# Two separate tiles for the odd pairs' arrays, second products in another order, and weight units in 11 stages: one change to a performer-and-two-MoE kernel on Trainium2

## The chip, the cores and the metric

The kernel runs on one core of one Trainium2 chip. The metric is the device time of one execution in microseconds (us). The core's engines run their own instruction streams and meet through semaphores: PE (TensorE, matrix products; PEld is its weight load), DVE (VectorE), ACT (ScalarE), POOL (GpSimd) and SP (SyncE, which here issues the transfers).

## The reference

What is computed, cut to what matters:

```python
attn = performer_attention(q, k, v, omega)            # 4 x 8 heads x 576 tokens x 64
x = attn.transpose(0, 2, 1, 3).reshape(2304, 512)
h = x @ w_in                                          # 512 -> 2048
x = (max(h, 0) + alpha * min(h, 0)) @ w_out           # first layer, 2048 -> 512
h = x @ w2_in
out = max(h, 0) ** 2 @ w2_out                         # second layer, same sizes
```

All is fp32. The matrix unit is used with operands rounded to a shorter format (`fp32r`), so each fp32 operand is kept as a rounded part (names with `h`) and a remainder (names with `l`), and a product is made of three matmuls: h x h, h x l and l x h.

## The kernel before

**Tiling.** The attention comes first and leaves `x` (512 x 2304) in memory. Then 2304 tokens are taken as three blocks of 768, each block as two halves of 384 (`HB`). The 2048 features are eight pairs of 128-row tiles. A *turn* is one pair of one block of the first layer.

**First products.** In block 0 of the first layer, `plain(p)` makes the four (feature half i, token half l) results of a pair in eight steps, one `multiply` (6 matmuls of 384 columns) each. From block 1 on, `pair(layer, p)` makes them in seven steps, with a scheme of seven products on sums of the quarters (`PRODUCTS`). It adds the seven products up in two PSUM arrays, `a` and `b`: products 1, 6, 7, 4 go to `a`, products 2, 5, 3 to `b`. Between them ACT copies `a` out (`copied`), and DVE adds such a copy to `b` (`plus`, tile `c`).

**Features.** The results pass through `activate` (first layer; ACT makes `n` and `r`, DVE puts them together with the slope `alpha`) or `square` (second layer). What follows is deferred: each step calls `catch_up()` once, which works off a list `behind` in stages. First comes "high": DVE computes the value and ACT rounds it into `gh`, at the next `catch_up`. Then comes "low": DVE makes the remainder `gl`, one `catch_up` later. All engines take their instructions in the order in which the code issues them.

**Second products of the first layer.** `mm2` multiplies the features of a turn with `w_out` during the next turn, in eight parts (half i = 1 first, four column groups c each); each part is 6 matmuls, of 512 and 256 columns. `FILL` says how many parts go behind each step m. The results add up over the eight turns of a block in six PSUM banks `y`, which `evacuate` empties when a block has ended (`COMPLETE` says which banks a part completes).

**Weights.** They arrive as 64-bit words and must be scaled, shifted, merged (ACT, DVE, POOL), summed for the seven-product scheme (`sums`), rounded (`cast1`, `cast2`, `cast3`) and given remainders (`rest1` to `rest3`), and are then written to HBM (`keep`) for the later blocks. The generator `made` does this in *units*: nine of the first layer, during the attention and block 0, and 16 of the second layer, eight each during blocks 1 and 2. Each unit is 18 stages (`STAGES`), and `upto` advances through them at a steady rate, behind each step of a turn: for the second layer's units 8 x 18 = 144 stages over the 49 steps of seven turns.

**The second layer.** `pair1` runs the seven products in an order in which product 1 of the next pair stands between 7 and 4. Even pairs take two tiles `h` for `a` and `b`; odd pairs take two banks of the tile `sumb`. The later `outer_products` (the second products of this layer, also with seven products) use `suma`, `sumb` and `sumc` as their sums; `combine` adds such a sum to `x` on DVE.

```python
a, b = (mp["ph"].tile([P, 512], F32, name="h")[:, :HB] for _ in range(2)) if p % 2 == 0 else (
    sums_of["b"][:, j, :HB] for j in range(2))
```

PSUM tiles and others are opened from pools with `reuse_waits="tile"`; the order of issue is written by hand, the waits are put in by the framework from the tiles that instructions read and write.

Of the kernel before, what the change touches and what calls it, by code (L numbers as in the profile page):

```python
# [9 lines left out]
F32 = mybir.dt.float32  # L10
# [8 lines left out]
P = 128  # L19
# [25 lines left out]
CAST = 11  # L45
STAGES = 18
DRAIN, DRAINED = 18, 6
# [5 lines left out]
def tile_performer_moe(ctx, tc, qt, kt, qn, kn, vn, omt, w1i, w1o, al, w2i, w2o, out):  # L53
# [100 lines left out]
    def made():  # L154
# [83 lines left out]
        for n, (n1, n2) in enumerate(UNITS):  # L238
            while n >= limit[0]:
                trail()  # L240
                yield
            todo = [[] for _ in range(STAGES)]
            if n1:

                plain = n1[0] == 0
                b0 = A21 if plain else A22
                a, b = used[n, 0, 0], used[n, 0, 1]
                todo[0] += [a.scale_high]
                todo[1] += [a.scale_low]
                todo[2] += [a.shift, b.scale_high]  # L250
                todo[3] += [lambda: merge(a), b.scale_low]
                todo[4] += [b.shift]
                todo[5] += [lambda: merge(b), lambda: cast1(n1, A11, S1)]
                todo[6] += [lambda: rest1(n1, A11, S1)]
                todo[7] += [lambda: cast1(n1, b0, A11)]
                todo[8] += [lambda: rest1(n1, b0, A11)]
                if not plain:
                    todo[8] += [lambda: keep(n1, 0, slice(0, 3), tiles["ma"])]
                todo[9] += [lambda: sums((1, 3))]
                todo[10] += [lambda: sums((2, 4))]  # L260
                todo[12] += [lambda: cast1(n1, S1, S3)]
                todo[13] += [lambda: rest1(n1, S1, S3), lambda: cast1(n1, S3, 8)]
                todo[14] += [lambda: rest1(n1, S3, 8)]
                if n == 0:
                    held.append(lambda n1=n1: keep(n1, 0, slice(0, 7), ring[0][0][:, :, A22:], nc.scalar))
                elif plain:
                    todo[14] += [lambda: keep(n1, 0, slice(0, 7), ring[n1[1] % 2][0][:, :, A22:])]
                else:
                    todo[14] += [lambda: keep(n1, 0, slice(3, 7), tiles["ms"])]
            todo[4] += [trail]  # L270
            todo[7] += [trail]
            if n2 and n2[0] == 1:
                a, b = used[n, 1, 1], used[n, 1, 0]
                todo[0] += [a.scale_high]
                todo[1] += [a.scale_low]
                todo[2] += [a.shift, b.scale_high]
                todo[3] += [lambda: merge(a), b.scale_low]
                todo[4] += [b.shift]
                todo[5] += [lambda: merge(b)]
                todo[7] += [lambda: sums((1, 3), True)]  # L280
                todo[8] += [lambda: sums((2, 4), True), lambda: cast3(0, 2)]
                todo[9] += [lambda: rest3(0, 2), lambda: cast3(2, 3)]
                todo[10] += [lambda: rest3(2, 3), lambda: keep3(n2[1], 0, 3)]
                todo[12] += [lambda: cast3(4, 6)]
                todo[13] += [lambda: rest3(4, 6), lambda: cast3(6, 8)]
                todo[14] += [lambda: rest3(6, 8), lambda: keep3(n2[1], 4, 8)]
            elif n2:
                raw = lambda i: used[n, 1, i]
                todo[8] += [lambda: raw(1).scale_high()]
                todo[9] += [lambda: raw(1).scale_low()]  # L290
                todo[10] += [lambda: raw(0).scale_high()]
                todo[11] += [lambda: raw(1).shift(), lambda: raw(0).scale_low()]
                todo[12] += [lambda: merge(raw(1))]
                todo[14] += [lambda: cast2(n2, 1)]
                todo[15] += [lambda: rest2(n2, 1)]
                todo[16] += [lambda: raw(0).shift()]
                todo[17] += [lambda: merge(raw(0)),
                             lambda: tail.extend([lambda n2=n2: cast2(n2, 0), lambda n2=n2: rest2(n2, 0)])]
            for stage in todo:
                for what in stage:  # L300
                    what()
                position[0] += 1
                yield
# [11 lines left out]
    making, fetches, stepping, held = [], [], [], []  # L315

    def onward(most, blk):

        ask(most, blk)
        next(making[0])  # L320

    def upto(where, most, blk):

        while position[0] < min(where, most * STAGES):
            onward(most, blk)
# [383 lines left out]
    def features(layer, p):  # L709
# [9 lines left out]
        def activate(i, l, c, psum=False):  # L719
# [9 lines left out]
            if halves[i][2] < 2:  # L729
                return  # L730

            def high():
                nc.vector.scalar_tensor_tensor(out=r, in0=n, scalar=al_sb[:, f:f + 1], in1=r, op0=ALU.mult, op1=ALU.add)  # L733
                nc.scalar.copy(out=gh[:, i], in_=r)  # L734
# [3 lines left out]

            behind[0].append((high, low))

        def square(i, l, c, psum=False):
# [5 lines left out]

            def high():
                if psum:
                    nc.vector.tensor_tensor(out=to, in0=r, in1=r, op=ALU.mult)  # L750
                else:
                    nc.vector.scalar_tensor_tensor(out=to, in0=c, scalar=0.0, in1=c, op0=ALU.max, op1=ALU.mult)
                if i and l:
                    nc.scalar.copy(out=g["h", p // 4][:, p % 4], in_=to)
# [5 lines left out]

            behind[0].append((high, low))

# [66 lines left out]

    behind = [[], []]  # L830

    def catch_up():

        high, low = behind
        for _, f in low:
            f()
        for f, _ in high:
            f()
        behind[:] = [], high

    def mm2(turn, p, gh, gl, y):

        w = ring[p % 2][1]
        for n, i in enumerate((1, 0)):
            first, last = turn == 0 and n == 0, turn == NPAIR - 1 and n == 1
            wh, wl = w[:, 0, i], w[:, 1, i]
            for c in range(KC):
                cs = slice(c * P, (c + 1) * P)
                for a0, a1 in cuts(c):
                    ts = slice(a0 - c * NB, a1 - c * NB)  # L850
                    for j, (u, v) in enumerate(((wh, gh), (wh, gl), (wl, gh))):
                        nc.tensor.matmul(  # L852
                            y[a0 // 512][:, a0 % 512:a0 % 512 + a1 - a0], u[:, cs], v[:, i, ts],
                            start=first and j == 0 and a0 % 512 == 0, stop=last and j == 2,
                            skip_group_check=True)
                yield

# [18 lines left out]

    FILL = {0: (0, 1, 1, 0, 3, 1, 2), 1: (0, 2, 2, 0, 3, 2, 3)}

    COMPLETE = {4: (0,), 5: (1, 2), 6: (3,), 7: (4, 5)}

# [25 lines left out]
    for n, (layer, k, turn, p) in enumerate(plan):  # L906
# [10 lines left out]
        for m, got in enumerate(steps, DRAINED if n == 0 else 0):  # L917
# [5 lines left out]
            if first and turn:  # L923

                upto((p + 1) * STAGES + STAGES * (m + 1) // 8 + 1, ENDS[0], 0)
            elif layer == 0 and k and turn:
                upto(ENDS[k - 1] * STAGES + 8 * STAGES * ((turn - 1) * 7 + m + 1) // 49, ENDS[k], k)
            elif layer == 0 and k and m == 6:
                ask(ENDS[k], k)
            elif (layer, k, turn) == (0, 1, 0) and m < 2:  # L930

                onward(ENDS[0], 0)
# [11 lines left out]
            full = []  # L944
            for _ in range(1 if first else FILL[layer][m]):
                part, _ = next(fill, (None, None))
# [18 lines left out]
    pz = ctx.enter_context(tc.tile_pool(name="pz", bufs=1, space=PSUM, reuse_waits="tile"))  # L965
    sums_of = {n: pz.tile([P, 2, 512], F32, name=f"sum{n}") for n in "bac"}
    ORDER = ((4, "c"), (1, "a"), (5, "b"), (6, "a"), (2, "c"), (7, "a"), (3, "c"))

    STATES = {4: (1, 1), 1: (0, 0), 5: (1, 1), 6: (1, 1), 2: (1, 0), 7: (0, 1), 3: (1, 0)}
    spread = {name: t.rearrange("p b n -> p (b n)")[:, :NB] for name, t in sums_of.items()}  # L970

    def slot_of(k, use):
        return (15 * k + use) % 2

    def pair1(k, p):

        a, b = (mp["ph"].tile([P, 512], F32, name="h")[:, :HB] for _ in range(2)) if p % 2 == 0 else (
            sums_of["b"][:, j, :HB] for j in range(2))
        w = ring[slot_of(k, p)][0]
# [35 lines left out]
    def outer_products(k, q, part, c_major=False, banks=None):  # L1015
# [3 lines left out]
        fresh = n not in (6, 7)  # L1019
        to = banks or [spread[name][:, c * QW:(c + 1) * QW] for c in range(3)]  # L1020
        h, l = g["h", part], g["l", part]
# [43 lines left out]
    def combine(k, n, name):  # L1065
        nc.vector.tensor_tensor(out=room_of(k, n), in0=spread[name], in1=room_of(k, n), op=ALU.add)  # L1066

# [63 lines left out]
    for k in range(BLOCKS):  # L1131
# [22 lines left out]
        for q in range(7):  # L1154
            for part in range(2):
# [10 lines left out]
                if (q, part) == (0, 0):  # L1166
                    for _ in range(2):
                        catch_up()
# [56 lines left out]
```

## Time and profile before

| | |
|---|---|
| time, median of 3 runs | 976.93 us (974.57 to 978.13) |
| the profiled execution | 975.11 us, span of its instructions 973.3 us |
| PE busy | 910.4 us, 94% of the span |
| DVE / ACT / POOL busy | 677.9 / 521.6 / 128.7 us |
| mean granted clock of TensorE | 0.993 |

Busy times of PE overlap, since matmuls are pipelined and their ends modelled: a matmul of 384 columns has a row of 0.34 us, while the next one can start after about half of that. A row of the profile gives the start in us from the span's start, the duration, the engine, the line of the kernel, the operation, what it writes and reads, and in brackets the idle time of the engine before it with the instruction that ended it. A row of a window gives its bounds and length, the busy us of PE, PEld, DVE, ACT and POOL with the number of their instructions, the granted clock, the busy share of the DMA engines and their GB/s.

The attention takes about the first 130 us; block 0 of the first layer lasts until about 270, blocks 1 and 2 until about 555, and the second layer takes the rest.

### The profile page before, as it was taken

The numbers are of one execution on the slowest core, as the hardware profiler recorded it, in microseconds if no ns is written. First come the engines' busy times: TensorE is split into PE (matmuls) and PEld (weight loads), VectorE is DVE, ScalarE is ACT, GpSimd is POOL, SyncE is SP. The second block draws the span as 40 slices with busy tenths as digits, with TensorE's granted clock in tenths as the row PEclk, the third lists the DMA queues.
The fourth block names the chain that finished last, engine by engine and source line by source line (L and its number), as shares of the span: only waits on it lengthen the run. The fifth ranks groups of instructions, "written<-read, shape, count | busy, mean of one in ns | idle before, by whom it ended". The sixth has DMA issues, their size and how long they took to land.

```text
span 973.3 us, 18463 instructions
## 1 busy us (share of the span) xinstructions
PE 910.4 (94%) x7328; PEld 834.2 (86%) x7328; DVE 677.9 (70%) x1071; ACT 521.6 (54%) x1109; POOL 128.7 (13%) x128
## 2 busy tenths in 40 slices
PE   9999999999999989899989888999988899988997
PEld 7998889888888878778878778889987899887997
DVE  5768878989877676776777754668745588446573
ACT  6888867767766665566665632235322245222341
POOL 6632203223101102101111100000000000000000
PEclk9999999999999999999999989999999999999999
DMA  8633336787558999548899655576776486865663
GB/s 296 198 106 114 111 141 214 262 290 280 187 184 290 325 344 351 182 172 322 302 360 351 252 184 176 181 270 250 252 246 211 156 310 220 298 202 179 271 250 108
DMA packets 81861, 228.81 MB, mean 235 GB/s; under 512 B 6128, under 2 KB 16752, under 8 KB 76400
## 3 DMA queue, kind: packets, MB, share of 16 engines
q1 hardware_dynamic: 81424, 225.77, 65.6%
q10 hardware_dynamic: 352, 1.87, 0.5%
q8 instruction: 58, 0.95, 0.4%
q14 instruction: 27, 0.22, 0.1%
HBM read 170.47 MB, written 57.15 MB: 234 GB/s over the span
## 4 chain that ended last, share of the span: by engine, by line
PE 45%; DVE 18%; ACT 15%; issue 4%; POOL 2%; DMA 2%; POOLq 0%; ACTq 0%; DVEq 0%
PE h L696 12%; PE sumb L696 9%; PE suma L1031 8%; PE sumc L1031 8%; PE y L852 5%; DVE r L733 4%; ACT gh L734 3%; PE sumb L1031 3%; ACT x L121 2%; DVE gl L737 2%; POOL wf L133 2%; DVE c L989 2%; ACT n L727 2%; ACT r L728 2%; DMA k<-ma 2%
## 5 line engine op out<-in xcount | busy, mean ns | idle before, releaser
L696 PE MATMUL h<-xh,w 128*128 128x384 f32 x1040 | 301.9, 341 | 12.6 <-DVE c L794 6.1
L696 PEld LDWEIGHTS h<-xh,w 128*128 128x128 f32 x1040 | 191.6, 189 | 26.2 <-DVE c L794 10.2
L852 PE MATMUL y<-gh,w 128*128 128x512 f32 (+1 forms) x768 | 212.5, 339 | 1.1 <-ACT gh L734 1.1
L696 PE MATMUL h<-xl,w 128*128 128x384 f32 x520 | 175.7, 338 | 0.9 <-DVE xl L374 0.9
L852 PEld LDWEIGHTS y<-gh,w 128*128 128x128 f32 x768 | 135.5, 189 | 15.9 <-DVE w L197 2.0
L852 PE MATMUL y<-gl,w 128*128 128x512 f32 (+1 forms) x384 | 132.2, 344 | 16.3 <-DVE gl L737 16.2
L133 POOL TENSOR_TENSOR wf<-x 128x512 int32<-128x512 int32 x64 | 79.3, 1240 | 367.1 <-DVE x L131 265.6
L696 PE MATMUL sumb<-xh,w 128*128 128x384 f32 x336 | 104.5, 358 | 24.9 <-DVE c L989 7.9
L1045 ACT CAST gh<-g 128x768 fp32r<-128x768 f32 x72 | 56.6, 833 | 84.9 <-PE suma L1031 38.7
L696 PEld LDWEIGHTS h<-xl,w 128*128 128x128 f32 x520 | 98.1, 189 | 4.5 <-DVE xl L374 1.4
L696 PEld LDWEIGHTS sumb<-xh,w 128*128 128x128 f32 x336 | 63.4, 193 | 39.8 <-DVE c L989 15.6
L852 PEld LDWEIGHTS y<-gl,w 128*128 128x128 f32 x384 | 72.5, 189 | 28.1 <-DVE gl L737 23.1
L1047 DVE TENSOR_TENSOR gl<-g,gh 128x768 fp32r<-128x768 f32 x72 | 65.8, 955 | 32.2 <-PE suma L1031 17.2
L734 ACT CAST gh<-r 128x768 fp32r<-128x768 f32 x48 | 40.1, 836 | 87.4 <-DVE r L733 87.4
L989 DVE TENSOR_TENSOR c<-sumb,s 128x384 f32<-128x384 f32 x24 | 13.4, 558 | 71.2 <-ACT s L985 45.4
L1031 PE MATMUL sumc<-w,gh 128*128 128x256 f32 x416 | 62.1, 286 | 0.0
L1031 PE MATMUL suma<-w,gh 128*128 128x256 f32 x448 | 58.1, 285 | 2.4 <-DVE x L1066 2.4
L478 DVE TENSOR_REDUCE mx<-h 128x8 f32<-128x1024 f32 x36 | 44.1, 1224 | 21.6 <-PE h L465 21.1
L1031 PEld LDWEIGHTS suma<-w,gh 128*128 128x128 f32 x448 | 55.9, 193 | 2.6 <-DVE x L1066 2.6
L696 PE MATMUL sumb<-xl,w 128*128 128x384 f32 x168 | 57.7, 343 | 0.0
L1031 PEld LDWEIGHTS sumc<-w,gh 128*128 128x128 f32 x416 | 57.2, 194 | 0.0
L131 DVE SCALAR_TENSOR_TENSOR x<-x,t 128x512 int32<-128x512 int32 x64 | 51.4, 803 | 1.7
(104 smaller groups left out, 1544.1 us busy)
## 6 DMA issues: line engine op xcount, KB each, us to landing
w<-k SPq DMA_DIRECT2D x93, 512.0 KB, 5.1
w<-k SPq DMA_DIRECT2D x42, 1024.0 KB, 4.7
w<-k SPq DMA_DIRECT2D x26, 896.0 KB, 8.1
k<-ms SPq DMA_DIRECT2D x16, 1024.0 KB, 6.4
k<-w SPq DMA_DIRECT2D x7, 1792.0 KB, 6.2
k<-ma SPq DMA_DIRECT2D x16, 768.0 KB, 5.1
x<-in_w1i SPq DMA_DIRECT2D x16, 512.0 KB, 4.3
x<-in_w1o SPq DMA_DIRECT2D x16, 512.0 KB, 3.9
```

The lines of the kernel that those rows point to most:

```text
L121: nc.scalar.mul(out=self.high.bitcast(F32), in_=self.high.bitcast(F32), mul=2.0 ** -112)
L131: nc.vector.scalar_tensor_tensor(out=self.high, in0=self.high, scalar=-0x80000000, in1=self.t, op0=ALU.bitwise_and, op1=ALU.bitwise_or)
L133: nc.gpsimd.tensor_tensor(out=self.out.bitcast(I32), in0=self.high, in1=self.low, op=ALU.add)
L478: nc.vector.reduce_max(out=mx, in_=pj, axis=AX.X)
L696: nc.tensor.matmul(out, w[:, u, a, cs], tiles[v, b][:, kc], start=start and kc == 0 and j == 0, stop=stop and kc == 1 and j == 2, skip_gro ...
L733: nc.vector.scalar_tensor_tensor(out=r, in0=n, scalar=al_sb[:, f:f + 1], in1=r, op0=ALU.mult, op1=ALU.add)
L734: nc.scalar.copy(out=gh[:, i], in_=r)
L852: nc.tensor.matmul(y[a0 // 512][:, a0 % 512:a0 % 512 + a1 - a0], u[:, cs], v[:, i, ts], start=first and j == 0 and a0 % 512 == 0, stop=las ...
L989: nc.vector.tensor_tensor(out=c, in0=b, in1=kept_[n], op=ALU.add)
L1031: nc.tensor.matmul(to[c], (l if v == 2 else h)[:, r, c * P:(c + 1) * P], w[:, rr, v % 2], start=fresh and rr == 0 and v == 0 and (c != 1 o ...
L1045: nc.scalar.copy(out=h[:, r], in_=f[:, r])
L1047: nc.vector.tensor_tensor(out=l[:, r], in0=f[:, r], in1=h[:, r].bitcast(F32), op=ALU.subtract)
```

## The change

1. The tile `sumb` of two banks becomes two tiles `spare[0]` and `spare[1]` of one bank each. Odd pairs take them as `a` and `b`; the outer products use them as sum "b" through `places`; `combine` of "b" becomes two instructions.
2. `catch_up` has three stages: the value (DVE), the rounding (ACT), the remainder (DVE), each one `catch_up` behind the other. Before the outer products it is called three times instead of two.
3. `mm2` has ten parts: for half i = 1 the matmuls with `gh` for each c (4 of 512 and 256 columns), then those with `gl` in two parts of two c each, then half i = 0 as before. `FILL` and `COMPLETE` follow. `FILL[0]` now serves block 0, `FILL[1]` all the rest.
4. Units of the second layer have 11 stages (`SHORT`) with the same instructions in tighter stages: 88 stages over 49 steps. Units of the first layer keep 18.

The diff, cut to its core:

```diff
-STAGES = 18
+STAGES, SHORT = 18, 11
...
+            layer = (n1 or n2)[0]
+            todo = [[] for _ in range((STAGES, SHORT)[layer])]
+            if layer:
+                a, b = (used[n, 0, 0], used[n, 0, 1]) if n1 else (used[n, 1, 1], used[n, 1, 0])
+                todo[0] += [a.scale_high]
+                todo[1] += [a.shift, a.scale_low]
+                todo[2] += [lambda: merge(a), b.scale_high]
+                todo[3] += [b.shift, b.scale_low]
+                todo[4] += [lambda: merge(b)]
+                todo[7] += [lambda: sums((1, 2), not n1)]
+                todo[8] += [lambda: sums((3, 4), not n1)]
+                if n1:
+                    todo[4] += [lambda: cast1(n1, A11, S1)]
+                    todo[5] += [lambda: rest1(n1, A11, S1), lambda: cast1(n1, A22, A11)]
+                    todo[6] += [lambda: rest1(n1, A22, A11), lambda: keep(n1, 0, slice(0, 3), tiles["ma"])]
+                    todo[8] += [lambda: cast1(n1, S1, S3)]
+                    todo[9] += [lambda: rest1(n1, S1, S3), lambda: cast1(n1, S3, 8)]
+                    todo[10] += [lambda: rest1(n1, S3, 8), lambda: keep(n1, 0, slice(3, 7), tiles["ms"])]
...
+    def end_of(n):
+        return min(n, NPAIR + 1) * STAGES + max(n - NPAIR - 1, 0) * SHORT
...
-        while position[0] < min(where, most * STAGES):
+        while position[0] < min(where, end_of(most)):
...
+            def slope():
+                nc.vector.scalar_tensor_tensor(out=r, in0=n, scalar=al_sb[:, f:f + 1], in1=r, op0=ALU.mult, op1=ALU.add)
             def high():
-                nc.vector.scalar_tensor_tensor(out=r, in0=n, scalar=al_sb[:, f:f + 1], in1=r, op0=ALU.mult, op1=ALU.add)
                 nc.scalar.copy(out=gh[:, i], in_=r)
...
-            behind[0].append((high, low))
+            behind[0].append((slope, high, low))
...
-    behind = [[], []]
+    behind = [[], [], []]
     def catch_up():
-        high, low = behind
-        for _, f in low:
-            f()
-        for f, _ in high:
-            f()
-        behind[:] = [], high
+        made_, rounded, left = behind
+        for one in left:
+            one[2]()
+        for one in rounded:
+            one[1]()
+        for one in made_:
+            one[0]()
+        behind[:] = [], made_, rounded
     def mm2(turn, p, gh, gl, y):
         w = ring[p % 2][1]
...
+        wh, wl = w[:, 0], w[:, 1]
+        head, tail = ((wh, gh), (wl, gh)), ((wh, gl),)
+        parts_ = [(1, (c,), head) for c in range(KC)] + [(1, (c, c + 1), tail) for c in (0, 2)]
+        parts_ += [(0, (c,), head + tail) for c in range(KC)]
...
-    FILL = {0: (0, 1, 1, 0, 3, 1, 2), 1: (0, 2, 2, 0, 3, 2, 3)}
+    FILL = ((1, 1, 1, 2, 2, 1, 1, 1), (0, 1, 2, 0, 4, 1, 2))
-    COMPLETE = {4: (0,), 5: (1, 2), 6: (3,), 7: (4, 5)}
+    COMPLETE = {6: (0,), 7: (1, 2), 8: (3,), 9: (4, 5)}
...
-                upto(ENDS[k - 1] * STAGES + 8 * STAGES * ((turn - 1) * 7 + m + 1) // 49, ENDS[k], k)
+                upto(end_of(ENDS[k - 1]) + 8 * SHORT * ((turn - 1) * 7 + m + 1) // 49, ENDS[k], k)
...
-            for _ in range(1 if first else FILL[layer][m]):
+            for _ in range(FILL[0 if first else 1][m]):
...
-    sums_of = {n: pz.tile([P, 2, 512], F32, name=f"sum{n}") for n in "bac"}
+    spare = [pz.tile([P, 512], F32, name=f"sumb{j}") for j in range(2)]
+    sums_of = {n: pz.tile([P, 2, 512], F32, name=f"sum{n}") for n in "ac"}
...
+    places["b"] = [spare[0][:, :QW], spare[0][:, QW:], spare[1][:, :QW]]
...
-            sums_of["b"][:, j, :HB] for j in range(2))
+            t[:, :HB] for t in spare)
...
+        o = room_of(k, n)
+        for what, at in [(spare[0], slice(0, 512)), (spare[1][:, :QW], slice(512, NB))] if name == "b" else [(spread[name], slice(0, NB))]:
+            nc.vector.tensor_tensor(out=o[:, at], in0=what, in1=o[:, at], op=ALU.add)
...
-                    for _ in range(2):
+                    for _ in range(3):
                         catch_up()
```

The units of the second layer's second weights are treated in the same way in the branch behind `if n1`, with `cast3`, `rest3` and `keep3`; `square` is split like `activate`, its first part being named `power`.

## Rows read from the trace of the kernel before

**Rows 1.** the page's busy times: us (share of the span) xinstructions
```profile
PE 910.4 (94%) x7328; PEld 834.2 (86%) x7328; DVE 677.9 (70%) x1071; ACT 521.6 (54%) x1109; POOL 128.7 (13%) x128
```

**Rows 2.** waits of PE, whole span: total us, times, longest
```profile
PE y L852 <- DVE gl L737: 16.2, 16, 2.8
PE sumb L696 <- DVE c L989: 7.9, 12, 0.7
PE sumb L696 <- ACT s L985: 7.3, 12, 0.6
PE sumb L696 <- ACT r L746: 7.0, 12, 0.6
...
PE h L696 <- DVE c L989: 1.4, 2, 0.7
```

**Rows 3.** timeline of PE around the second layer's odd pair 1, block 1
```profile
709.61 0.33 PE L696 MATMUL h<-xh,w 128*128 128x384 f32 x1
...
711.69 0.34 PE L696 MATMUL sumb<-xh,w 128*128 128x384 f32 x1
...
712.55 0.34 PE L696 MATMUL sumb<-xh,w 128*128 128x384 f32 x1
713.54 0.44 PE L696 MATMUL sumb<-xh,w 128*128 128x384 f32 x1 [0.65 <-DVE c L989]
713.82 0.34 PE L696 MATMUL sumb<-xl,w 128*128 128x384 f32 x1
```

**Rows 4.** an even and an odd pair: busy us (instructions), clock, DMA share, GB/s
```profile
720.90:738.56 17.66, 15.70 (x85) 14.42 (x85) 8.32 (x16) 4.78 (x10) 0.00 (x0) 1.00 0.65 209
```

**Rows 5.** timeline of PE in the first odd pair, and a window within
```profile
574.23 0.33 PE L696 MATMUL sumb<-xh,w 128*128 128x384 f32 x1
...
577.15 0.44 PE L696 MATMUL sumb<-xh,w 128*128 128x384 f32 x1 [1.71 <-ACT n L985]
...
590.40 0.34 PE L696 MATMUL h<-xh,w 128*128 128x384 f32 x1
...
577.00:586.00 9.00, 7.56 (x24) 6.74 (x25) 1.44 (x3) 0.58 (x2) 0.00 (x0) 0.62 0.30 89
```

**Rows 6.** the page's DMA issues: count, KB each, us to landing
```profile
w<-k SPq DMA_DIRECT2D x93, 512.0 KB, 5.1
```

**Rows 7.** waits of PE from 285 to 565 us
```profile
PE y L852 <- DVE gl L737: 11.7, 9, 2.8
PE h L696 <- DVE c L794: 6.1, 10, 1.0
PE h L696 <- ACT s L789: 4.5, 6, 1.2
PE y L852 <- ACT gh L734: 1.1, 2, 0.5
```

**Rows 8.** windows of one turn, and behind the longest wait
```profile
450.60:467.70 17.10, 16.03 (x90) 14.02 (x88) 11.64 (x22) 11.82 (x24) 3.12 (x3) 1.00 0.96 338
...
541.00:545.00 4.00, 4.00 (x16) 3.82 (x17) 3.02 (x5) 3.18 (x6) 0.00 (x0) 0.57 0.96 293
```

**Rows 9.** timeline at the end of that turn
```profile
464.07 0.84 ACT L734 CAST gh<-r 128x768 fp32r<-128x768 f32 x1 [1.50 <-DVE r L733]
...
465.33 0.51 PE L696 MATMUL h<-xh,w 128*128 128x384 f32 x2
...
466.54 0.40 PE L852 MATMUL y<-gh,w 128*128 128x512 f32 x1
...
466.78 0.46 ACT L789 COPY s<-h 128x384 f32<-128x384 f32 x1
...
467.70 0.50 PE L852 MATMUL y<-gl,w 128*128 128x512 f32 x1 [0.76 <-DVE gl L737]
```

**Rows 10.** window of one turn of block 0, and DVE's waits over four
```profile
180.54:198.59 18.05, 17.35 (x97) 15.65 (x97) 16.37 (x23) 12.56 (x24) 5.32 (x4) 1.00 0.78 277
...
DVE w L197 <- ACT w L194: 4.7, 8, 0.9
```

More of the change, by code (lines that the diff above doesn't have):

```diff
@@ L241, in made @@
                 yield
[L242 to L246, printed above, removed]
+            layer = (n1 or n2)[0]
[16 more added lines that the diff above has]
+                    todo[10] += [lambda: rest1(n1, S3, 8), lambda: keep(n1, 0, slice(3, 7), tiles["ms"])]
+                else:
+                    todo[4] += [lambda: cast3(0, 2)]
+                    todo[5] += [lambda: rest3(0, 2), lambda: cast3(2, 3)]
+                    todo[6] += [lambda: rest3(2, 3), lambda: keep3(n2[1], 0, 3)]
+                    todo[8] += [lambda: cast3(4, 6)]
+                    todo[9] += [lambda: rest3(4, 6), lambda: cast3(6, 8)]
+                    todo[10] += [lambda: rest3(6, 8), lambda: keep3(n2[1], 4, 8)]
+            elif n1:
                 a, b = used[n, 0, 0], used[n, 0, 1]
@@ L254, in made @@
                 todo[6] += [lambda: rest1(n1, A11, S1)]
[L255 to L258, printed above, removed]
+                todo[7] += [lambda: cast1(n1, A21, A11)]
+                todo[8] += [lambda: rest1(n1, A21, A11)]
                 todo[9] += [lambda: sums((1, 3))]
@@ L265, in made @@
                     held.append(lambda n1=n1: keep(n1, 0, slice(0, 7), ring[0][0][:, :, A22:], nc.scalar))
-                elif plain:
+                else:
                     todo[14] += [lambda: keep(n1, 0, slice(0, 7), ring[n1[1] % 2][0][:, :, A22:])]
[L268 to L287, printed above, removed]
+            if not layer:
+                todo[4] += [trail]
+                todo[7] += [trail]
+            if n2 and not layer:
                 raw = lambda i: used[n, 1, i]
@@ L746, in square, with power @@
                 nc.scalar.activation(out=r, in_=c, func=AF.Relu)
-            def high():
+            def power():
                 if psum:
@@ L752, in high @@
                     nc.vector.scalar_tensor_tensor(out=to, in0=c, scalar=0.0, in1=c, op0=ALU.max, op1=ALU.mult)
+            def high():
                 if i and l:
@@ L759, in low @@
                                             op=ALU.subtract)
-            behind[0].append((high, low))
+            behind[0].append((power, high, low))
         return gh, gl, square if layer else activate
@@ L827, in pair @@
         yield gh, gl
-    behind = [[], []]
+    behind = [[], [], []]
     def catch_up():
-        high, low = behind
-        for _, f in low:
-            f()
-        for f, _ in high:
-            f()
-        behind[:] = [], high
+        made_, rounded, left = behind
[6 more added lines that the diff above has]
+        behind[:] = [], made_, rounded
     def mm2(turn, p, gh, gl, y):
         w = ring[p % 2][1]
[L844 to L848, printed above, removed]
+        wh, wl = w[:, 0], w[:, 1]
+        head, tail = ((wh, gh), (wl, gh)), ((wh, gl),)
+        parts_ = [(1, (c,), head) for c in range(KC)] + [(1, (c, c + 1), tail) for c in (0, 2)]
+        parts_ += [(0, (c,), head + tail) for c in range(KC)]
+        for n, (i, cs, what) in enumerate(parts_):
+            first, last = turn == 0 and n < KC, turn == NPAIR - 1 and n >= KC + 2
+            for c in cs:
                 for a0, a1 in cuts(c):
                     ts = slice(a0 - c * NB, a1 - c * NB)
-                    for j, (u, v) in enumerate(((wh, gh), (wh, gl), (wl, gh))):
+                    for j, (u, v) in enumerate(what):
                         nc.tensor.matmul(
-                            y[a0 // 512][:, a0 % 512:a0 % 512 + a1 - a0], u[:, cs], v[:, i, ts],
+                            y[a0 // 512][:, a0 % 512:a0 % 512 + a1 - a0], u[:, i, c * P:(c + 1) * P], v[:, i, ts],
                             start=first and j == 0 and a0 % 512 == 0, stop=last and j == 2,
                             skip_group_check=True)
-                yield
+            yield
     def cuts(c):
@@ L970, in tile_performer_moe @@
     spread = {name: t.rearrange("p b n -> p (b n)")[:, :NB] for name, t in sums_of.items()}
+    places = {name: [t[:, c * QW:(c + 1) * QW] for c in range(3)] for name, t in spread.items()}
+    places["b"] = [spare[0][:, :QW], spare[0][:, QW:], spare[1][:, :QW]]
     def slot_of(k, use):
@@ L1019, in outer_products @@
         fresh = n not in (6, 7)
-        to = banks or [spread[name][:, c * QW:(c + 1) * QW] for c in range(3)]
+        to = banks or places[name]
         h, l = g["h", part], g["l", part]
@@ L1065, in combine @@
     def combine(k, n, name):
-        nc.vector.tensor_tensor(out=room_of(k, n), in0=spread[name], in1=room_of(k, n), op=ALU.add)
+        o = room_of(k, n)
+        for what, at in [(spare[0], slice(0, 512)), (spare[1][:, :QW], slice(512, NB))] if name == "b" else [(spread[name], slice(0, NB))]:
+            nc.vector.tensor_tensor(out=o[:, at], in0=what, in1=o[:, at], op=ALU.add)
     def store(k, n, l, j):
```

## The prediction

> **What bounds the kernel now.** First the engines' busy times: TensorE is busy 94% of the span [rows 1]. The other engines matter only where TensorE waits for them, so the next view is the list of TensorE's waits [rows 2]. It has a striking set of three rows: matmuls into `sumb` wait twelve times each for DVE `c` (L989), ACT `s` (L985) and ACT `r` (L746). There are twelve odd pairs in the second layer (1, 3, 5, 7 in each of three blocks), so each wait occurs once per odd pair. The same code on the even pairs, whose two arrays are separate tiles `h`, waits for `c` twice in the whole run [rows 2].
>
> The timeline of one odd pair shows what a wait costs [rows 3]. Undisturbed, twelve matmuls of 384 columns take from 709.61 to 711.69: 0.173 us each. The last matmul of product 2 starts at 712.55, so product 6 could start at 712.72. It starts at 713.54, and the matmul after it comes 0.28 later instead of 0.17. Lost: 0.82 + 0.10 = 0.92, where the idle column shows 0.65. **So a wait costs its idle time plus about 0.27**: busy times overlap by about 0.17, and the restart costs 0.10. I use this surcharge throughout.
>
> Is the wait real? Product 6 adds into array `a`; `c` is computed from array `b`. Nothing that product 6 writes is read by that DVE instruction. The two arrays are halves of one tile, and the release goes by tile. The same holds for product 5 (`b`) behind ACT's copy of `a`, and for product 3 (`b`) behind ACT's read of `a`. Even pairs, with the same order but two tiles, show none of this.
>
> **Part 1: two tiles for the odd pairs.** Two pairs, an even and an odd one, take 17.66 us [rows 4]. They hold 14 products of 6 matmuls: 84 x 0.173 = 14.56. The difference is 3.1 us, all in the odd pair. Eight odd pairs are of this full kind (p = 3, 5 of the first block, p = 1, 3, 5 of the other two): 8 x 3.1 = 24.8. Pair 7 has no product 1 of a next pair and so only the three listed waits: (7.9 + 7.3 + 7.0)/12 + 3 x 0.27 = 2.66, three times: 8.0.
>
> The first odd pair of the layer is worse [rows 5]. From 574.23 to 590.40 it runs 8 products, 48 x 0.173 = 8.3 us of work, in 16.17 us: 7.9 lost. Product 2 waits 1.71 for ACT's copy of the other array, and afterwards the granted clock averages 0.62 from 577 to 586, which is mostly the lower level. With two tiles product 2 starts at 575.27 and ends near 576.3. Product 6 writes the copied array and must wait until the copy, held up by evacuations, ends near 577.1: 0.8 + 0.3 remain. Gain 6.8.
>
> What could be late next in these pairs? DVE is busy 8.32 us of 17.66 and ACT 4.78 [rows 4]: over 14.56 that is 57% and 33%. The weights are read into the slot of the pair before last, by transfers that land 5.1 us after their issue in the median [rows 6]. Between the last use of an array and its next use there are about ten products, 10.4 us, after the change too. The DMA share of 0.65 becomes 0.65 x 17.66/14.56 = 0.79, below the 0.96 that other stretches show [rows 8]. So nothing takes the waits' place. The added cost, `combine` of the "b" sums as two DVE instructions instead of one, six more in all, runs during the outer products with DVE off the path: nothing; uncovered it would be about 0.2 us each. **Sum of part 1: 24.8 + 8.0 + 6.8 = 39.6 us**; bounds 37 (the first pair gains half, the copies come later) and 41.
>
> **Part 2: blocks 1 and 2 of the first layer** (16 turns from 285 to 565, the last beside the second layer's first pair). TensorE's waits there are 9 on `gl` (11.7 us), 2 on `gh` (1.1), 10 on `c` (6.1) and 6 on `s` (4.5) [rows 7]. With 0.27 each: 14.1 + 1.6 + 8.8 + 6.1 = 30.6. The longest, 2.67, is followed by 4 us at a granted clock of 0.57 [rows 8]: 4 x (1 - 0.57) = 1.7. In all 32.3.
>
> Three edits act here. *The order of the second products*: the rounded features `gh` of half i = 1 are used first (at step m = 1), the remainders `gl` only at step 4. `gl` is written one step later than before and used some three steps later, so the `gl` waits go (14.1), and the lower clock behind the longest with them (1.7). *The third stage of `catch_up`*: before, ACT's cast stood directly behind DVE's slope, and ACT held everything behind it (1.50 at 464.07 [rows 9]) while DVE worked. Now slope, cast and remainder each get a step. But the cast of half i = 1 thereby moves behind ACT's copy `s` of product 1. That is a new wait: in rows 9 product 1's last matmul starts at 465.33 and ends near 465.67; the copy takes 0.46 and the cast 0.84, so `gh` is there at about 467.0, while TensorE reaches the first second product at 466.54. New loss: 0.5 + 0.1 = 0.6 in each of 16 turns, 9.6 us. Before, the `gl` instruction of the same place started at 467.70.
>
> The waits on `c`: the remainder of half 1 (0.95 on DVE) no longer stands ahead of `c` at step 1, and 1.4 us of heads instead of one full part of 1.04 stand between it and its user. All ten are at most 1.0 long, so nearly all go; I leave 1.8 of 8.8. The waits on `s` often follow a late `c`, and ACT no longer stands still at the slope; I leave 2.5 of 6.1. *The shorter, even stages*: the instructions are the same; per unit they are spread over 11 stages instead of 15 of 18, at 88 stages over 49 steps instead of 144. The cast behind the second merge now comes one stage after it instead of two, about the same time. Here the cover is thin: the DMA share is 0.96 in a turn of 17.10 us [rows 8]; a turn that shortens by 1 us raises it by a twentieth, and a read that is late is late for TensorE. I charge 2 us for it. The new losses: 9.6 + 1.8 + 2.5 + 2 = 16, so **part 2 gains 16**. Bounds: 26 if the copy and cast run hidden and the rest goes; 2 if the new `gh` wait becomes as long as the `gl` wait was.
>
> **Part 3: block 0.** Seven of the 16 waits on `gl` in rows 2 are here (16.2 - 11.7 = 4.5 us): 4.5 + 7 x 0.27 = 6.4. The new order removes them, for in this block the cast stands ahead of the activations and not behind a copy. But DVE is busy 16.37 us of a turn of 18.05, and waits 4.7 in four turns, 1.2 per turn, for ACT's cast of the weights [rows 10]. If those waits stay, a turn cannot be shorter than 17.57: 7 x 0.48 = 3.4. If the moved cast frees ACT and they go, TensorE's 96 x 0.173 = 16.6 and DVE's 16.4 allow the whole 6.4. **I take 5.**
>
> **The sum.** The profiled execution took 975.11 us, its span 973.3; the median of the runs is 976.93, 0.2% above. 39.6 + 16 + 5 = 60.6: a span of 912.7, a time of 914.5, rounded to 914. Half a per cent, 5 us, is about what this kernel's measurement can tell.
>
> **A rule against it.** The row of 541 to 545 shows this: after 2.67 us of waiting TensorE ran at the lower of its two levels, 1.2 GHz [rows 8]; the sixteen waits on `gl`, most of them shorter, left only this one such stretch. The Trainium skill ("TensorE: Matmul & The Clock Gate", section "HAM oscillation — how this bites in real kernels") says that a loop which leaves the array idle between bursts can fall back to the half rate in every round and pays for it every time. If the new `gh` wait did that, it would be the third rival below; by the row, waits of 0.6 do not.
>
> **The rivals.**
> 1. *Blocks 1 and 2 gain nothing*: copy and cast come so late, or the transfers so crowded, that the new waits add up to the old 32. For it: the DMA share of 0.96, and ACT's copy at 466.78, a microsecond later than its product allowed. Against it: ACT's 1.50 of standing still goes. Time 975.1 - 39.6 - 5 = 930. Chance 0.16.
> 2. *The split does not do what it says*: the odd pairs go on waiting, because the release goes by something wider than the tile. Against it: the even pairs. Time 975.1 - 16 - 5 = 954. Chance 0.04.
> 3. *Not faster*: in each turn of blocks 1 and 2 the new wait on `gh` grows to 2.7 us and the clock falls behind it, as once at 541: 2.67 + 0.27 + 1.7 = 4.6 a turn, 74 us in place of 32. Time 975.1 + 42 - 39.6 - 5 = 973, no change; slower by over 5 us from 5.1 a turn on. The wait would have to be five times what its two ACT instructions explain. Chance 0.02, half of it slower.
> 4. *Nearly all waits go*: part 2 gains 26 or more and part 3 6.4. Time 902 or less. Chance 0.12.
>
> My forecast has the rest, 0.66. The range runs from case 4's edge, 901, to case 1's, 931; case 2, case 3 and the far parts of 1 and 4 lie outside, under 0.2 together. Faster 0.98, the same 0.01, slower 0.01.
>
> **What would show it.** Waits of TensorE on `sumb` should be gone: two pairs in 14.6 us, no stretch of lower clock near 580. `y` should wait for ACT `gh` (L734's successor) about 16 times at 0.3 to 0.4 idle, and not for `gl`. ACT's cast `gh` should hardly wait for DVE `r` any more, as it did for 1.50 in rows 9. Block 0's turns should be near 17.3. The prediction is wrong if the second layer's pairs keep a period above 15 us, or if the stretch from block 1 to the second layer (285 to 565 in the trace of before) does not shorten by some 16 us.

## The result and the profile after

The changed kernel takes 914.9 us (median of 3 runs, 912.28 to 915.36) against 976.93: a ratio of 0.9361, 95% interval 0.9322 to 0.9400. The forecast was 914. The profiled execution has a span of 913.6 us, 59.7 less than before. How the 59.7 divide is read from the start times of three matmuls in the traces: the first of the first layer (129.41 us before, 129.60 after), the first second product that runs in block 1, which still belongs to block 0's last turn (270.47 and 262.79), and the first into the odd pairs' arrays in the second layer (574.23 and 549.12).

| stretch (us) | before | after | gain | forecast |
|---|---|---|---|---|
| until the first layer (attention) | 129.4 | 129.6 | -0.2 | 0 |
| block 0 | 141.1 | 133.2 | 7.9 | 5 |
| blocks 1 and 2 | 303.8 | 286.3 | 17.5 | 16 |
| second layer, from its first odd pair | 399.1 | 364.5 | 34.6 | 39.6 |

The sum was right, but two of its terms were off by 3 to 5 us in opposite directions. That the time came out within 1 us of 914 is therefore luck. The page's first line for PE answers to rows 1:

```profile
PE 891.6 (98%) x7328; PEld 832.2 (91%) x7328; DVE 676.6 (74%) x1077; ACT 523.5 (57%) x1109; POOL 130.9 (14%) x128
```

PE's waits over the whole span (total us, times, longest) answer to rows 2 and 7. The three rows on `sumb` are gone, and so are all waits on `gl`. Sixteen waits on `gh` stand in their place, as forecast, and small ones on `xl`, the operands' remainders, and on transfers:

```profile
PE y L867 <- ACT gh L743: 5.5, 16, 0.6
PE h L703 <- DVE xl L381: 3.2, 3, 2.0
PE h L703 <- DMA w<-k: 2.9, 4, 1.1
PE suma L1049 <- DVE x L1087: 2.4, 1, 2.4
PE h L703 <- DVE c L1007: 1.4, 2, 0.7
...
PE h L703 <- ACT s L800: 1.1, 3, 0.4
```

Two windows: an even and an odd pair, answering to rows 4, and a turn of block 0, answering to rows 10.

```profile
670.85:685.92 15.07, 15.07 (x86) 14.49 (x85) 8.03 (x16) 4.68 (x11) 0.00 (x0) 1.00 0.88 294
177.75:194.55 16.80, 16.80 (x98) 15.74 (x98) 15.56 (x23) 12.86 (x26) 4.92 (x5) 1.00 0.84 297
```

The pairs went from 17.66 to 15.07, not to 14.56. The turn of block 0 went from 18.05 to 16.80. The end of a turn in block 2, answering to rows 9:

```profile
463.10 0.48 ACT L800 COPY s<-h 128x384 f32<-128x384 f32 x1 [0.54 <-PE h L703]
...
463.47 0.84 ACT L743 CAST gh<-r 128x768 fp32r<-128x768 f32 x1
...
464.36 0.97 PE L867 MATMUL y<-gh,w 128*128 128x512 f32 x4 [0.31 <-ACT gh L743]
```

ACT no longer stands still for DVE's slope there. It waits for PE, copies, casts, and PE waits 0.31 for the cast: the chain of the forecast, link by link.

### The profile page after: what moved, and what is told of

It reads as the page before. It is cut to its first block, busy times and chain, and to the rows that moved or that the text cites. A ratio compares the mean times of both kernels' runs of the same rounds, so it can differ in the third digit from the quotient of the medians.

```text
span 913.6 us, 18523 instructions
## 1 busy us (share of the span) xinstructions
PE 891.6 (98%) x7328; PEld 832.2 (91%) x7328; DVE 676.6 (74%) x1077; ACT 523.5 (57%) x1109; POOL 130.9 (14%) x128
## 4 chain that ended last, share of the span: by engine, by line
PE 78%; DVE 9%; DMA 6%; ACT 4%; issue 2%; POOL 0%; SPq 0%; ACTq 0%; DVEq 0%
PE h L703 22%; PE y L867 14%; PE suma L1049 9%; PE sumb L703 8%; PE sumc L1049 8%; PE h L472 4%; DMA w<-k 4%; PE sumb L1049 3%; PE t L592 2%; PE o L624 2%; PE t L479 2%; PE o L518 2%; DVE r L740 2%; DVE xl L381 1%; DMA k<-ms 1%
## 5 line engine op out<-in xcount | busy, mean ns | idle before, releaser
L867 PE MATMUL y<-gh,w 128*128 128x512 f32 (+1 forms) x768 | 177.4, 339 | 5.5 <-ACT gh L743 5.5
L867 PEld LDWEIGHTS y<-gh,w 128*128 128x128 f32 x768 | 130.3, 188 | 22.0 <-ACT gh L743 10.6
L133 POOL TENSOR_TENSOR wf<-x 128x512 int32<-128x512 int32 x64 | 81.5, 1273 | 341.6 <-DVE x L131 140.8
L867 PE MATMUL y<-gl,w 128*128 128x512 f32 (+1 forms) x384 | 103.6, 338 | 0.0
L703 PE MATMUL sumb<-xh,w 128*128 128x384 f32 x336 | 93.7, 338 | 0.0
L867 PEld LDWEIGHTS y<-gl,w 128*128 128x128 f32 x384 | 67.5, 188 | 9.2
L740 DVE SCALAR_TENSOR_TENSOR r<-n,al_sb,r 128x768 f32<-128x768 f32 x48 | 57.2, 1191 | 1.5 <-ACT r L735 1.5
L746 DVE TENSOR_TENSOR gl<-r,gh 128x768 fp32r<-128x768 f32 x48 | 51.5, 1072 | 0.9 <-ACT gh L743 0.9
L805 DVE TENSOR_TENSOR c<-h,s 128x384 f32<-128x384 f32 x51 | 28.3, 555 | 30.1 <-PE h L703 22.8
```

Source lines behind the costliest of these rows:

```text
L133: nc.gpsimd.tensor_tensor(out=self.out.bitcast(I32), in0=self.high, in1=self.low, op=ALU.add)
L703: nc.tensor.matmul(out, w[:, u, a, cs], tiles[v, b][:, kc], start=start and kc == 0 and j == 0, stop=stop and kc == 1 and j == 2, skip_gro ...
L746: nc.vector.tensor_tensor(out=gl[:, i], in0=r, in1=gh[:, i].bitcast(F32), op=ALU.subtract)
L805: nc.vector.tensor_tensor(out=c, in0=b, in1=s, op=ALU.add)
L867: nc.tensor.matmul(y[a0 // 512][:, a0 % 512:a0 % 512 + a1 - a0], u[:, i, c * P:(c + 1) * P], v[:, i, ts], start=first and j == 0 and a0 % ...
```

## The experiments

The theory after the result: the tile alone made the waits in the second layer; in the first layer the new order and the third stage belong together, the shorter units are a small part, and the cast behind the copy is the price. The rivals were that one edit carries all, or that the named wait is not the cause.

**1. The two tiles alone**, put into the kernel before.

```diff
-    sums_of = {n: pz.tile([P, 2, 512], F32, name=f"sum{n}") for n in "bac"}
+    spare = [pz.tile([P, 512], F32, name=f"sumb{j}") for j in range(2)]
...
-            sums_of["b"][:, j, :HB] for j in range(2))
+            t[:, :HB] for t in spare)
```

> The kernel before with the two tiles for the odd pairs alone (and `combine` of the "b" sums in two instructions). Theory A, the waits on `sumb` come from the common tile: the three rows of twelve waits on `sumb` go, the second layer shortens by the 34.6 us by which it shortened under the whole change (399.1 to 364.5 from the first matmul into `sumb` to the end), and the time is 976.9 - 34.6 = 942, give or take 2. The first layer stays as it was. Theory B, the second layer's gain came from the three-stage catch-up, which moves DVE's and ACT's work out of the way: the waits on `sumb` stay and the time is within 3 us of 977.

Measured 941.7 us, 0.9642 (0.9595 to 0.9689) of before. Theory A holds. PE's waits there:

```profile
PE y L852 <- DVE gl L737: 16.0, 16, 2.8
...
PE sumb L696 <- ACT n L988: 0.7, 1, 0.7
```

The `sumb` rows of rows 2 are gone but for one wait of 0.7 in the first odd pair, which the forecast had left there; the waits on `gl` stand. The second layer takes 361.6 us, 2.9 less than under the whole change, and its regular pairs take 7.28 us, exactly 42 x 0.1733. Blocks 1 and 2, though, take 306.0 us in this trace instead of 303.8, with the clock at its lower level in four stretches there instead of one. So the second layer gained 37.5 us and not the 34.6 of the expectation, and the time of 942 came out in part because the two differences offset each other.

**2. One tile again**, in the changed kernel: the same lines the other way round.

> The changed kernel with `sumb` as one tile again. Theory A (the tile alone makes the waits): the waits return in the old number, 36 of about 0.6 us, the second layer takes about 399 us again and the time is 914.9 + 34.6 = 949.5, give or take 3; the lower clock near the first odd pair may or may not come back (3 us of it). Theory B (the third stage of the catch-up made the gain): the time stays within 4 us of 915.

Measured 955.6 us, 0.9790 (0.9744 to 0.9836): 41 us more than the changed kernel, so theory A holds, but 6 us over its 949.5. The waits return, one of them longer than before, in PE's waits:

```profile
PE sumb L703 <- DVE c L1004: 11.8, 12, 1.0
PE sumb L703 <- ACT s L1000: 7.3, 12, 0.6
PE sumb L703 <- ACT r L755: 7.0, 12, 0.6
```

The wait on `c` has grown from 7.9 to 11.8 us, and the second layer takes 404.0, 4.9 more than before. The tile is the cause of these waits, and another edit makes DVE's `c` later. That is followed up in 6 and 7.

**3. The old order of the second products**, with the changed kernel's three stages and units.

```diff
-        parts_ = [(1, (c,), head) for c in range(KC)] + [(1, (c, c + 1), tail) for c in (0, 2)]
-        parts_ += [(0, (c,), head + tail) for c in range(KC)]
+        for n, i in enumerate((1, 0)):
...
+                    for j, (u, v) in enumerate(((wh, gh), (wh, gl), (wl, gh))):
```

> The changed kernel with the second products in the old order (eight parts, all three matmuls of a column group together, the old numbers of parts behind each step). Theory A, the reordering pays for the third stage: `gl` of half 1 is now written at the catch-up of step 1 and needed right behind it, so each of the 16 turns of blocks 1 and 2 waits about 2 us instead of 0.6, and each of block 0's seven about 1: 16 x 1.4 + 7 x 1 = 29 us, a time of 944, between 930 and 955. Theory B, the order does not matter because stages and catch-up alone made the gain in the first layer: 915 to 920.

Measured 946.9 us, 0.9692 (0.9641 to 0.9743): theory A. PE's waits, then one of them in PE's timeline and the window behind it:

```profile
PE y L865 <- DVE gl L746: 22.5, 17, 2.5
PE y L865 <- ACT gh L743: 6.6, 16, 1.1
```
```profile
488.47 0.79 PE L865 MATMUL y<-gl,w 128*128 128x512 f32 x1 [2.46 <-DVE gl L746]
```
```profile
488.50:491.90 3.40, 3.40 (x11) 3.21 (x12) 2.55 (x6) 1.11 (x3) 0.00 (x0) 0.50 0.97 310
```

In the window the clock is at the lower of its two levels. Eight such stretches lie in blocks 1 and 2 of this run, each begun within 1.5 us of the end of a `gl` wait of 1.2 to 2.5 us; the turns with `gl` waits of 0.8 to 1.1 kept the full clock. The mean granted clock is 0.984 instead of 0.998: 947 x 0.016 less 914 x 0.002 makes some 13 us of clock lost more. The third stage without the new order makes blocks 1 and 2 slower than they were before, 315.8 us instead of 303.8. Block 0 it makes faster, 135.4 us instead of 141.1, only 2.2 more than the whole change; the expectation had charged 7 there. The edit takes back `FILL` with the order, so the order of the matmuls and the steps that they stand behind were not separated.

**4. Slope and cast in one stage again**, first layer only.

```diff
-            def slope():
+            def high():
                 nc.vector.scalar_tensor_tensor(out=r, in0=n, scalar=al_sb[:, f:f + 1], in1=r, op0=ALU.mult, op1=ALU.add)
-            def high():
                 nc.scalar.copy(out=gh[:, i], in_=r)
...
-            behind[0].append((slope, high, low))
+            behind[0].append((high, low))
```

> The changed kernel with the first layer's slope and cast in one stage again (the second layer keeps three). Theory A: the wait of TensorE on `gh`, 16 times 0.58 us, goes, since the cast stands before the copy again (9 us gained); against it ACT stands still at the slope again, 1.5 us a time, so its copies come late: waits on `s` of 6 to 9 us return, and block 0 loses about 0.5 us in each of seven turns. Sum about 916, between 909 and 923: the third stage by itself is worth little. Theory B, the third stage is what freed the first layer: over 925.

Measured 935.5 us, 0.9576 (0.9532 to 0.9621). Theory A fell, and theory B holds. The waits on `gh` went as it said, but what came back was far more than 6 to 9 us: block 0 takes 140.1 us and blocks 1 and 2 302.4, within 1.4 us of before. PE's waits (those on `w` are all in block 0), and below them the row of ACT's here and under the whole change:

```profile
PE h L703 <- ACT s L798: 11.1, 14, 1.9
PE h L703 <- DVE c L803: 8.2, 8, 1.6
PE y L863 <- DVE w L197: 5.2, 6, 1.0
```
```profile
ACT gh L741 <- DVE r L740: 81.2, 46, 3.1
```
```profile
ACT gh L743 <- DVE r L740: 16.5, 13, 2.9
```

The rows fit this account: while ACT stands at the slope, the copies and weight casts behind it are late, then DVE's `c` and weight remainders, and PE meets them one after the other.

**5. The units in 18 stages again.** The branch for the second layer's units is that of before, and `SHORT` is 18.

> The changed kernel with the second layer's weight units in their old 18 stages, three with nothing in them, 144 stages over the 49 steps. Theory A, the even stages are a small part: the same instructions come in denser bursts, some waits on ACT `s` and DVE `c` return, 2 to 6 us, a time of 919 (914 to 923). Theory B, the even spread made most of the 17.4 us of blocks 1 and 2: 926 or more.

Measured 920.9 us, 0.9431 (0.9412 to 0.9449): theory A, 6 us, all in blocks 1 and 2 (292.5 us).

**6. The addition ahead of the catch-up**, where pairs meet in the second layer.

```diff
-            catch_up()
+            if n != 3:
+                catch_up()
```

> The changed kernel without the catch-up behind the last product (3) of each pair of the second layer; its work is done at the next step, behind DVE's addition `c` of product 2. Theory A: the 0.24 us that each pair still loses ahead of product 5 comes from DVE, where a remainder and a power stand ahead of `c`. It goes in about 21 pairs: 5 us, a time of 910 (908 to 912), two pairs in 14.6 us instead of 15.08. Theory B: the loss is the length of the chain product 2, `c`, product 5 itself: nothing changes, 914 to 916.

Measured 911.7 us, 0.9333 (0.9316 to 0.9350). In its trace the regular pairs take 7.28 to 7.32 us instead of 7.53, and the second layer 361.1 instead of 364.5: theory A, with 3.4 us instead of 5. The times of 6 to 8 lie only 3 us below 914.9, whose own three runs span 912.28 to 915.36; these gains are read from the stretches of the traces. DVE's timeline of the whole change shows what 6 removed, and PE's row what it had cost:

```profile
672.08 0.56 DVE L1007 TENSOR_TENSOR c<-h,s 128x384 f32<-128x384 f32 x1 [1.46 <-PE h L703]
672.56 0.55 DVE L769 TENSOR_TENSOR gl<-g,gh 128x384 fp32r<-128x384 f32 x1
673.02 0.55 DVE L759 TENSOR_TENSOR g<-r 128x384 f32<-128x384 f32 x1
673.49 0.55 DVE L1007 TENSOR_TENSOR c<-sumb,n 128x384 f32<-128x384 f32 x1
```
```profile
673.79 0.75 PE L703 MATMUL sumb<-xh,w 128*128 128x384 f32 x2
```

A remainder (`gl`) and a power (`g`) stand between the last `c` of one pair and the first of the next. The second `c` ends at 674.04, and product 5, which writes `sumb` next, starts at 674.10 instead of 673.96, and the matmul after it 0.28 later instead of 0.17. That is 0.24 us, and too short for the list of waits.

**7. The second layer's features in two stages**, the first layer's in three.

```diff
-            behind[0].append((power, high, low))
+            behind[0].append((high, low))
```

> The changed kernel with the second layer's features in two stages again (power and cast together, remainder one step later), the first layer in three. Theory A, the third stage is what keeps the second layer's pairs at 7.53 us instead of 7.28, because remainder and power stand together ahead of DVE's addition `c`: pairs of 7.28 us as in the run with the two tiles alone, the second layer 361.6 instead of 364.5, a time of 912 (910 to 913). Theory B, the pairs are slower because something else of the whole change reaches into them (transfers, the first layer's rest): 914 to 916.

Measured 912.4 us, 0.9329 (0.9306 to 0.9352). Pairs of 7.28 us, a second layer of 361.1: theory A. Two pairs in a window, against the 15.07 above:

```profile
663.90:678.50 14.60, 14.60 (x87) 14.60 (x86) 8.38 (x16) 4.69 (x10) 0.00 (x0) 1.00 0.86 291
```

**8. The cast ahead of the copy** in step 0 of a turn.

```diff
         product(a, 1, True)
-        s = copied()
         catch_up()
+        s = copied()
```

> The changed kernel with one line moved: in step 0 of a turn of seven products the catch-up is issued ahead of ACT's copy of product 1, so the cast into `gh` no longer stands behind a copy that waits for TensorE. Theory A, the copy in front of the cast makes the wait on `gh`: its 16 waits (0.31 idle, 0.58 lost) go, 16 x 0.58 = 9.3 us, a time of 906, at least 909 if ACT's copy, now behind the cast, is late in a few turns. Theory B, the slope on DVE comes too late for the cast anyway: the waits stay and the time with them, 913 to 917.

Measured 911.7 us, 0.9332 (0.9314 to 0.9350). Theory A was right on the wait and wrong on its worth. The `gh` waits fell from 16 to 3 (0.6 us), but blocks 1 and 2 gained 4.2 us, not 9.3: PE's waits on ACT's copy `s` there rose from 1.1 us (3) to 3.8 (7). ACT's timeline before one of them, and PE's row:

```profile
316.40 0.40 ACT L194 CAST ma<-wf 128x256 fp32r<-128x256 f32 x1 [1.65 <-POOL wf L133]
...
316.71 0.47 ACT L800 COPY s<-h 128x384 f32<-128x384 f32 x1
...
317.24 0.44 PE L703 MATMUL h<-xh,w 128*128 128x384 f32 x1 [0.64 <-ACT s L800]
```

The copy stands behind a weight cast that waits for POOL. That the short wait on `gh` had let ACT keep up at such places is inferred; no run shows it.

**9. The moves of 6 and 8 together; those of 7 and 8 together; and a better order of preparation.**

> Both moves together, cast ahead of the copy in the first layer and addition ahead of the catch-up in the second. If both theories A hold, 915 - 9.3 - 5 = 901 (899 to 905); if only one does, 906 or 910.

> As the last, with the cast ahead of the copy in step 0 of a turn. The two gains lie in different layers and should add: 914.9 - 3 - 3.2 = 909 (907 to 911).

Measured 909.3 us (0.9311, 0.9292 to 0.9330) and 910.1 (0.9317, 0.9298 to 0.9336). The first missed its 901 by about what 6 and 8 had missed; the second came out as expected. The last kernel adds to the second of them the operands of product 7 ahead of those of product 4:

```diff
-            4: ..., 5: [(rest, T1)], 6: [(difference, T4)],
-            7: [(difference, T3), (cast, T4)], 8: [(rest, T4), (cast, T3)], 9: [(rest, T3), (cast, B22)],
+            4: ..., 5: [(rest, T1)], 6: [(difference, T3)],
+            7: [(difference, T4), (cast, T3)], 8: [(rest, T3), (cast, T4)], 9: [(rest, T4), (cast, B22)],
```

> As the last, with the operands of product 7 (T3) prepared one step ahead of those of product 4 (T4) instead of behind them, in blocks 1 and 2 and for the second layer. Theory A: TensorE's longest wait in the first layer, 2.4 us for the remainder of T3 in the turn beside the second layer's first pair, and the like one of 1.0 at the start of block 2, come from this order; 2 to 4 us go, a time of 906. Theory B: DVE as a whole is behind at these places and T4, or product 3, waits in its place: 909.

Measured **903.5 us, 0.9243 (0.9223 to 0.9263)**, faster than both kernels of this study. PE's waits on `xl` fell from 3.6 us to this:

```profile
PE h L703 <- DVE xl L381: 0.5, 2, 0.3
```

Of the 6.7 us between the medians, 3.1 are those waits. The profiled executions lie only 3.8 us apart (908.0 and 904.23), at a mean granted clock of 0.998 each. The other four executions of the kernel without the new preparation had 0.994 to 0.996, those of the last one 0.998 or 1.0: most of the rest goes with the clock. That the new preparation keeps the clock up was not shown.

## Why the prediction was right, point by point

**Part 1, the two tiles: the mechanism right, the size 5 us too large.** Experiments 1 and 2 show it from both sides, and rival 2 (a release wider than the tile) is out. The step that failed is the floor of 84 x 0.173 = 14.56 with "nothing takes the waits' place". That floor is real: experiment 1 runs at it. But under the whole change two pairs took 15.07, since the third stage of `catch_up` also applies to the second layer, and there it puts a remainder and a power ahead of `c`. The prediction priced the third stage in the first layer only. By its own sign, a period above 15 us, this part failed by a little, though no wait on `sumb` is listed and the clock near 580 is full. The trace has twenty places like the one at 674.10, of 0.24 us each: 4.9 us. Experiments 6 and 7 remove them and give back 3.4 each; meanwhile the waits of `sumc` on transfers of weights grew there from 0.7 us to 2.0 and 2.1.

**Part 2, blocks 1 and 2: the new wait right, the sum of 17.5 against 16 partly luck.** The new wait on `gh` was priced at 0.6 in each of 16 turns, 9.6 us. Measured: 5.5 of idle time and 16 x 0.27, 9.8. The waits on `gl` and on `c` went altogether; those on `s` kept 1.1 idle. Transfers took 2.9 idle, 4.0 with a surcharge of 0.27 for each of the four, where 2 had been charged. Not foreseen were 3.2 us on `xl`, of which 0.9 had been there before. With the surcharge the listed waits sum to about 20 where 16 had been forecast. Before, the same list has 34.6 with the lower clock, two waits on `xl` and one more on `s` than the prediction counted; the difference is some 15 of the 17.5. The rest are waits too short for the list. Six of them in the trace of before are like this one, where two matmuls start 0.36 apart instead of 0.17 because ACT's copy `s` ends at 310.30; with the matmul behind them they make some 1.7 us:

```profile
309.99 0.80 PE L696 MATMUL h<-xh,w 128*128 128x384 f32 x2
310.63 0.33 PE L696 MATMUL h<-xl,w 128*128 128x384 f32 x1
```

ACT's cast, which was hardly to wait for `r` any more, still does so 13 times for 16.5 us, against 46 times for 87.4 before. One expectation formed after the result was wrong: that the third stage is worth little. With the order but not the stage the first layer gains 2.4 us, with the stage but not the order it loses 6, with both it gains 25 (experiments 3 and 4, beside the short units).

**Part 3, block 0: 7.9 against 5, beyond the bound of 6.4.** With the moved cast ACT is freer, and DVE's waits for weight casts fell from 4.7 us in four turns to this:

```profile
DVE w L197 <- ACT w L194: 2.8, 4, 1.3
```

PE waits for nothing in these turns any more, and a turn is its own 96 matmuls, 16.80 us; the 16.6 of the prediction took 0.173 us throughout, and those of 512 columns start about 0.23 apart. The step that failed is the bound: it counted the waits on `gl` alone, 6.4 us, while short ones on the weights' remainders `w` went too. They are too short for the list. Before, in five turns, a matmul like the one at 171.40 starts 0.12 to 0.15 late, as DVE's second remainder ends at 171.35, and the next one another 0.11:

```profile
171.02 0.40 PE L852 MATMUL y<-gl,w 128*128 128x512 f32 x1
171.40 0.62 PE L852 MATMUL y<-gh,w 128*128 128x512 f32 x2
```

That is 1.2 us. The prediction also gave the gain to the new order, with the moved cast as a condition. The runs have it the other way round: with the third stage and the old order block 0 gains 5.7 us (experiment 3), with the new order and two stages 1.0, since waits of PE on `w` of 5.2 us come in place of those on `gl` (experiment 4).

**The rivals.** Rival 1 (nothing in blocks 1 and 2) is what happens without the third stage: 302.4 us. Rival 3 (the clock falls in each turn) did not come to the changed kernel, whose waits of 0.3 to 0.6 left the clock full; it came to experiment 3, in half of the turns. The rule of the Trainium skill that the prediction weighed ("TensorE: Matmul & The Clock Gate", section "HAM oscillation — how this bites in real kernels": a loop whose waits leave the array idle can start each round at the lower clock) fits that run in eight of its 16 turns, and the changed kernel in none. Rival 4's time comes to 903 by its own terms (975.1 - 39.6 - 26 - 6.4), not to 902 or less; nothing else rests on it.

## What to carry to other kernels

Where two arrays are written and read in turn, look in the list of waits for a matmul that waits for a reader of the other array; if both are halves of one tile, try two tiles; here they removed the waits, and no cost of theirs showed. Do not put an engine's instruction directly behind another engine's result in an in-order queue when other work stands behind it: give each its own step, and move the user of the result back by as much, since here the one without the other gained 2.4 us or lost 6, and both together 25. And price such a stage in every place that calls it, also where the old distance had been just right.

## What the runs showed of the hardware that was not expected

DVE's instructions in a turn of block 0 are the same 23 before and after, but their busy time fell from 16.37 to 15.56 us. In DVE's groups over four turns of the changed kernel:

```profile
L746 DVE TENSOR_TENSOR gl<-r,gh 128x768 fp32r<-128x768 f32 x9 | 12.0, 1328 | 0.0
L740 DVE SCALAR_TENSOR_TENSOR r<-n,al_sb,r 128x768 f32<-128x768 f32 x8 | 11.2, 1403 | 0.0
L131 DVE SCALAR_TENSOR_TENSOR x<-x,t 128x512 int32<-128x512 int32 x16 | 11.0, 690 | 0.4
L128 DVE TENSOR_SCALAR t<-x 128x512 int32<-128x512 int32 x16 | 6.7, 419 | 0.4
```

Before, these four took 949, 1009, 870 and 622 ns in the mean: the instructions that take longer have changed places. In these four turns of either trace, these differ from the others in which of two overlapping instructions, DVE's or POOL's addition (L133), started first. Of the DVE instructions that recur, all 31 that take over 5% longer than the shortest of their kind start while a POOL addition is under way; the 24 beside which POOL started later, and the 121 with none beside them, are within those 5%. One pair from each trace, the slope behind POOL's start after and ahead of it before:

```profile
177.37 1.53 POOL L133 TENSOR_TENSOR wf<-x 128x512 int32<-128x512 int32 x1 [3.98 <-ACT x L121]
...
177.92 1.80 DVE L740 SCALAR_TENSOR_TENSOR r<-n,al_sb,r 128x768 f32<-128x768 f32 x1
```
```profile
181.47 1.01 DVE L733 SCALAR_TENSOR_TENSOR r<-n,al_sb,r 128x768 f32<-128x768 f32 x1
...
181.79 1.60 POOL L133 TENSOR_TENSOR wf<-x 128x512 int32<-128x512 int32 x1 [5.81 <-DVE x L131]
```

The change moved the starts against each other. The Trainium skill ("SBUF — State Buffer", section "Who interferes with whom") has DVE and GpSimd take turns at a shared port when a DVE instruction reads two inputs from SBUF, or runs in a mode that uses both of its ports. The traces fit that. In blocks 1 and 2 the addition `c`, which reads one of its inputs from PSUM, ran ten times beside a POOL addition that had started earlier, and took 0.54 to 0.56 us, as it does alone. No run was made to separate it.
